# One burst for the next batch's packed product and two packed blocks, its columns inside an h tile

## The chip, the core and the metric

The kernel runs on one core of one Trainium2 chip. The metric is device time in microseconds of one execution; the median of three runs is 249.57 (249.48 to 250.11). The engines named below are TensorE (PE, with its weight loads PEld), VectorE (DVE), ScalarE (ACT), GpSimd (POOL) and SyncE (SP).

## The reference

Eight batches, eight heads, 576 positions, head size 64, 32 packed queries, a feed-forward layer of 512 to 2048 to 512:

```python
p_packed = sm_attn(p, k, v)                # softmax attention of 32 packed queries
out = sm_attn(q, p_packed, p_packed)       # attention of q over the 32 packed rows
x = out.transpose(0, 2, 1, 3).reshape(B * S, H * D)
h = x @ w_in
g = h * cos(h)
return g @ w_out
```

`sm_attn(qq, kk, vv)` is `softmax(scale * qq kk^T) vv`.

## The kernel before

For one batch `b` the kernel makes, in order:

- `s1(b)` (L142): scores of the packed queries against k, in two PSUM tiles, and their exp on ACT. `a1_xbar` (L158) or `a1_pe` (L163) transposes the result, `recips` (L152) takes reciprocals of its sums.
- `pp(b)` (L173), the packed product: 48 small matmuls (96 rows, 32 columns, 64 wide; L180) into 128 columns of a PSUM tile, and two copies to `pp_sb` in SBUF. `pp_T(b)` (L188) transposes it on PE (L192) and copies it to `ppT`, which has a buffer for each parity of `b`.
- `ppw(b, n)` (L195), a packed block: 8 matmuls (64 rows, 32 columns, 512 wide; L207) that multiply `ppT` by columns `512n` to `512n+511` of `w_in`, into both banks of a PSUM tile, and a cast into `PPW[b]` (L85 on ACT, L87 on DVE). There are four blocks, n = 0 to 3; `pw2(b, n)` (L485) makes two. Folding `w_in` into the packed rows spares the product `x @ w_in`.
- `s2(b)` (L221): scores of q against the packed rows (L137), exp on ACT (L225). `sums2` (L228) sums them with a matmul by ones and takes the logarithm; `normalise` (L238) makes the weights `a2n`.
- `h_mm(b, fc)` (L248) for fc = 0 to 15: one h tile, four matmuls (L254) of a 128-column piece of `PPW[b]` with `a2n[b]`. Its PSUM tile has two banks of 512 columns, of which each holds 288 (HS) used columns. ACT makes the cosine as a sine (L258), DVE multiplies (L261) into `gT`. The tiles of fc 4n to 4n+3 read block n.
- `out_gen(b)` (L331): `g @ w_out`, in chunks of 16 matmuls each (L339), whose result is copied to `osb` and stored by an SP DMA (L345). It is a generator: `fill(n)` (L355) issues its next n matmuls wherever it is called. These are the fillers, always those of the batch before. An odd batch has 80, an even one 64.

The whole order is written out by hand (a manual schedule): an instruction stands in its engine's queue where the program calls it. PE, ACT and DVE each run their queue in order.

`slot(s, hooks, keep, heavy)` (L471) is the h loop of batch s. It issues the 16 h tiles, spreads the fillers between them, and calls each hook after the h tile whose number it carries. An fc in `heavy` gets more fillers, half of them before its hook and half after.

PSUM has two single-bank buffers for the output tiles (pool `psO`, tile `ot`) and, from batch 1 on, three two-bank buffers (pool `psA`, `psa()`, L89) that score tiles, h tiles, packed products, transposes and packed blocks take in turn. A tile can be taken only when its buffer's last reader is done.

The bursts of small tiles in the loop over s = 3 to 6 (L545) are four for each batch: after `s2(s)` comes `ppw(s, 2)`; after `s1(s+1)` comes `ppw(s, 3)`; inside the slot, `pp(s+1)` stands after fc 5, with `pp_T(s+1)` after fc 6; and `pw2(s+1)`, blocks 0 and 1 of the next batch, after fc 10. The last batch, s = 7, has only its own two blocks. Batches 1 and 2 have slots of their own (L496, L542).

The diff touches `h_mm`, the hooks of the slots, and the calls around `pp(2)` and in the loop.

Of the kernel before, what the change touches and what calls it, by code (L numbers as in the profile page):

```python
# [15 lines left out]
def kernel(  # L16
# [18 lines left out]
    HS = S // 2  # L35
# [27 lines left out]
    V, ACT, G = nc.vector, nc.scalar, nc.gpsimd  # L63
# [25 lines left out]
    def psa(dt=FP32):  # L89
        return psum["A"].tile([128, 2, 512 if dt == FP32 else 1024], dt, name="psA", tag="A")  # L90
# [29 lines left out]
    def pack_p(b0, b1, flat=None):  # L120
        ng = 2 * (b1 - b0)
        if flat is None:
            flat = psa(BF16).rearrange("p a x -> p (a x)")
        for g in range(ng):
            nc.tensor.transpose(flat[:, g * 128:(g + 1) * 128],
                                p_bf[:, 2 * b0 + g].rearrange("p t d -> p (t d)"), ident)
        V.tensor_copy(out=P2[:, b0:b1].rearrange("p b h n -> p (b h n)"), in_=flat[:, 0:ng * 128])
# [14 lines left out]
    def s1(b):  # L142
        ps = scores(lambda r, h, e: P2[r, b, h, :], xT["k", b])
        sm = small.tile([128, 2], FP32, name="sums1")
        for y in range(2):
            ACT.activation(  # L146
                out=a1[b % 2][:, y, :, 0:TP].rearrange("p (e m) x -> p e m x", e=2),
                in_=ps[y][:, :, 0:HS].rearrange("p e (m x) -> p e m x", m=3),
                func=AF.Exp, scale=scale, accum_out=sm[:, y:y + 1])
        sums1[b] = sm  # L150
# [22 lines left out]
    def pp(b, eng=V, own=None):  # L173

        ps = own() if own else psa()[:, 0, :]
        for y in range(2):
            for j in range(C):
                c = 2 * (j % 3) + j // 3
                for x in range(4):
                    nc.tensor.matmul(ps[32 * x:32 * x + 32, y * D:(y + 1) * D],  # L180
                                     a1T[b][0:TP, y, j, 32 * x:32 * x + 32],
                                     bf["v", b][:, 2 * x + y, c * D:(c + 1) * D],
                                     start=(j == 0), stop=(j == C - 1))
        t = pp_sb[b % 2].rearrange("p a d -> p (a d)")
        copy(eng, t[:, 0:2 * D], ps[:, 0:2 * D])
        copy(eng, t[:, 2 * D:3 * D], ps[:, 0:D])
# [8 lines left out]
    def ppw(b, n, eng=None, own=False, later=False, cuts=((0, 512),)):  # L195
        if b not in PPW:
            PPW[b] = ppw_pool.tile([128, 2, DF], BF16, name="PPW", tag="PPW")
        two = isinstance(eng, tuple)
        if own:
            ps = [bank(), bank()]  # L200
        else:
            t = psa()
            ps = [t[:, 0, :], t[:, 1, :]]
        for x in range(4):
            for y in range(2):
                r = slice(64 * y, 64 * y + 64)
                nc.tensor.matmul(ps[y][32 * x:32 * x + 32, :], ppT[b % 2][r, 0, x, :],  # L207
                                 w_in_bf[r, x, n * 512:(n + 1) * 512], start=True, stop=True)

        def evacuate(cuts=cuts):  # L210
            if own or two:
                for a, z in cuts:
                    for y in range(2):
                        copy(eng[y] if two else eng, PPW[b][:, y, n * 512 + a:n * 512 + z], ps[y][:, a:z])
            else:
                copy(eng or (V, ACT)[n % 2], PPW[b][:, :, n * 512:(n + 1) * 512], t)
        if later:
            return [lambda c=c: evacuate((c,)) for c in cuts]
        evacuate()
# [25 lines left out]

    gT, joint = {}, {}

    def h_mm(b, fc):  # L248
        if fc == 0:
            g_tile(b)  # L250
        ps = psa()
        for y in range(2):
            for e in range(2):
                nc.tensor.matmul(ps[:, e, 0:HS], PPW[b][:, y, fc * 128:(fc + 1) * 128],  # L254
                                 a2n[b][:, y, e * HS:(e + 1) * HS], start=(y == 0), stop=(y == 1))
        cs = cos_pool.tile([128, S], BF16, name="cosT")
        csv = cs.rearrange("p (e x) -> p e x", e=2)
        ACT.activation(out=csv, in_=ps[:, :, 0:HS], func=AF.Sin, bias=PI_HALF)  # L258

        def rest():  # L260
            V.tensor_tensor(out=gT[b][:, fc, :].rearrange("p (e x) -> p e x", e=2),  # L261
                            in0=ps[:, :, 0:HS], in1=csv, op=ALU.mult)
            if fc % 8 == 7:
                j0 = (b % 2) * 64
                G.tensor_copy(out=joint[b // 2][:, fc - 7:fc + 1, j0:j0 + 64],  # L265
                              in_=gT[b][:, fc - 7:fc + 1, 512:576])
        return rest
# [18 lines left out]
    def h_rest(b):  # L286

        t = psa()
        for fc in range(NFC):
            for y in range(2):  # L290
                nc.tensor.matmul(t[:, fc // 8, (fc % 8) * 64:(fc % 8) * 64 + 64],
                                 PPW[b][:, y, fc * 128:(fc + 1) * 128], a2n[b][:, y, 512:576],
                                 start=(y == 0), stop=(y == 1))
        cs = cos_pool.tile([128, 2, 512], BF16, name="cosR", bufs=1)
        ACT.activation(out=cs, in_=t, func=AF.Sin, bias=PI_HALF)
        j0 = (b % 2) * 64
        V.tensor_tensor(out=joint[b // 2][:, :, j0:j0 + 64],
                        in0=t.rearrange("p a (f x) -> p (a f) x", x=64),
                        in1=cs.rearrange("p a (f x) -> p (a f) x", x=64), op=ALU.mult)
# [55 lines left out]
    def fill(n):  # L355
        while n > 0 and filler[1] > 0:
            next(filler[0])
            filler[1] -= 1
            n -= 1
# [111 lines left out]
    def slot(s, hooks, keep=0, heavy={}):  # L471
        left = filler[1] - keep
        weight = [1 + heavy.get(fc, 0) for fc in range(NFC)]
        for fc in range(NFC):
            h_mm(s, fc)()
            quota = (left * sum(weight[:fc + 1])) // sum(weight) - (left + keep - filler[1])
            first = quota
            while hooks and hooks[0][0] == fc:
                if first == quota and fc in heavy:
                    first = quota // 2  # L480
                    fill(first)
                hooks.pop(0)[1]()
            fill(quota - first if first != quota else quota)

    def pw2(b, n=0, eng=None):  # L485
        ppw(b, n, eng)
        ppw(b, n + 1, eng)

    def tk(n, b, i):
        return lambda: pe_T(n, b, (ACT, V, ACT), (i,))  # L490

    def cross(n, b):
        return lambda: xbar(n, b)

    osb_eng[0] = ACT
    slot(1, [(2, lambda: ppw(1, 2, (ACT, V))), (4, lambda: h_rest(0)),  # L496
             (5, lambda: ppw(1, 3, (ACT, V))), (6, lambda: pack_p(2, 4)), (8, tk("k", 2, 0)), (9, tk("k", 2, 1)),
             (9, cross("q", 2)), (10, tk("k", 2, 2)), (12, cross("k", 3))], 4, {4: 2})
    ACT.preload_act_table_set(EXP_SET)
    osb_eng[0] = V  # L500
    G.tensor_copy(out=gate, in_=xT["k", 3][0:1, 0, 0:1])
# [11 lines left out]
    recips(2)  # L513
    fill(5)
    pp(2)
    fill(2)
    pp_T(2)
    s1(3)
    a1_xbar(3)
    recips(3)  # L520
    fill(6)
    s2(2)
# [15 lines left out]
    for n, b in (("v", 4), ("q", 4), ("k", 5)):  # L538
        load(n, b)
    fill(9)  # L540
    osb_eng[0] = ACT
    slot(2, [(3, lambda: ppw(2, 2, (ACT, V))), (6, lambda: ppw(2, 3, (ACT, V))),  # L542
             (7, lambda: pp(3, ACT)), (8, lambda: pp_T(3, ACT)), (11, lambda: pw2(3))], 5, {11: 3})

    for s in range(3, B):  # L545
        nxt = s + 1 < B
        ACT.preload_act_table_set(EXP_SET)
        osb_eng[0] = V
        fill(1000)
        set_filler(s - 1)  # L550
        s2(s)
        ppw(s, 2, V)
        fill(8)
        if nxt:
            s1(s + 1)
            ppw(s, 3, V)
            a1_xbar(s + 1)
            xbar("q", s + 1)
            recips(s + 1)
            if s + 2 < B:  # L560
                xbar("k", s + 2)
                G.tensor_copy(out=gate, in_=xT["k", s + 2][0:1, 0, 0:1])
        else:
            ppw(s, 3, V)
        fill(4)
        sums2(s, 0)
        fill(5)
        sums2(s, 1)
        normalise(s)
        ACT.preload_act_table_set(SIN_SET)  # L570
        fill(13)
        osb_eng[0] = ACT
        for n, b in (("v", s + 2), ("q", s + 2), ("k", s + 3)):
            if b < B:
                load(n, b)
        slot(s, [(5, lambda: pp(s + 1, ACT)), (6, lambda: pp_T(s + 1, ACT)), (10, lambda: pw2(s + 1))] if nxt else [], 5, {10: 3})
    set_filler(B - 1)
    fill(1000)
    tail_chunk(B - 1, 4)
# [30 lines left out]
```

## Time and profile before

| what | value |
|---|---|
| median of three runs | 249.57 us |
| the profiled execution | 249.53 us |
| its span on the core | 247.6 us |
| granted TensorE clock over the span | 1.0 |
| L339, fillers | 482 and 47 recorded matmuls, 128.2 and 12.6 us busy |
| L254, h tiles | 448 matmuls, 73.2 us busy |
| L207, packed blocks | 224 and 32 matmuls, 10.4 and 1.6 us busy |
| L180, packed products | 336 and 48 matmuls, 4.0 and 0.6 us busy |
| L258, the sine of one h tile | 653 ns |
| L261, the multiply of one h tile | 757 ns |
| L87, a cast of a whole packed block on DVE | 1223 ns |
| L85, the same on ACT | 1012 ns |

A profile row reads: start, duration, engine, line, operation, output tile from input tiles, shape, count of merged instructions, and in brackets the idle time of the engine before them with what ended it. The duration of a merged row runs from its first start to its last end. Ends of matmuls are modelled, since they are pipelined; the distance of starts is firmer. A few matmul records are missing from the trace. All times are microseconds from the start of the span.

### The profile page before, as it was taken

What the parts mean: (1) busy time and instruction counts of PE and PEld (TensorE: products, weight loads), DVE (VectorE), ACT (ScalarE), POOL (GpSimd) and SP (SyncE); (2) the same over time, 40 slices, a digit from 0 to 9 for tenths busy, and PEclk for the clock granted to TensorE, in tenths of its full rate; (3) what the DMA queues carried; (4) which work ended last, traced back from release to release, by engine and by line L of the source; (5) the groups of instructions that cost most, each with busy time, mean ns of one, the idle gap of its engine ahead of it and who ended that gap; (6) DMA issues with size and microseconds to landing.
All of it is one profiled execution on the core that took longest, in us unless ns stands there. A gap on an engine that the chain in (4) does not pass through costs nothing.

```text
span 247.6 us, 5423 instructions
## 1 busy us (share of the span) xinstructions
PE 234.0 (95%) x2204; PEld 128.3 (52%) x2240; DVE 158.5 (64%) x244; ACT 170.3 (69%) x284; POOL 38.2 (15%) x61
## 2 busy tenths in 40 slices
PE   7988889999989999999999999999999999999993
PEld 3453344566445554565446554565456554665452
DVE  3369977676549777578757666578756685774000
ACT  2369998677568777888787677978886685874110
POOL 8532330200400041005000500030000000000000
PEclk9999999999999999999999999999999999999999
DMA  6999999999899999996999894989292113111123
GB/s 88 204 209 209 202 208 228 202 235 176 135 186 173 218 146 201 189 221 122 215 214 197 148 222 109 184 172 203 63 187 59 42 45 84 43 34 53 52 75 85
DMA packets 63992, 37.37 MB, mean 151 GB/s; under 512 B 36592, under 2 KB 59376, under 8 KB 63968
## 3 DMA queue, kind: packets, MB, share of 16 engines
q0 software_dynamic: 23184, 18.81, 50.0%
q1 hardware_dynamic: 40624, 18.09, 35.6%
q8 instruction: 17, 0.28, 0.5%
q10 hardware_dynamic: 160, 0.13, 0.2%
q14 instruction: 7, 0.06, 0.1%
HBM read 37.22 MB, written 9.44 MB: 188 GB/s over the span
## 4 chain that ended last, share of the span: by engine, by line
PE 82%; DMA 6%; DVE 4%; ACT 3%; issue 2%; POOL 2%; DVEq 0%; ACTq 0%; POOLq 0%
PE ot L339 48%; PE psA L254 22%; DMA w_in_bf<-in_moe_w_in_dram 6%; PE psA L207 3%; PE psA L137 2%; PE ot L325 1%; PE psA L233 1%; PE psA L180 1%; DVE gT L284 1%; PE psH L280 1%; DVE PPW L87 1%; ACT a2u L225 1%; DVE gT L261 1%; POOL kbf L94 1%; ACT L449 1%
## 5 line engine op out<-in xcount | busy, mean ns | idle before, releaser
L339 PE MATMUL ot<-w_out_bf,gT 128*128 128x512 bf16 x482 | 128.2, 379 | 2.8 <-issue 1.9
L261 DVE TENSOR_TENSOR gT<-psA,cosT 128x576 bf16<-128x576 f32 x112 | 83.5, 757 | 32.4 <-ACT cosT L258 31.5
L258 ACT ACTIVATE cosT<-psA 128x576 bf16<-128x576 f32 x112 | 73.0, 653 | 26.4 <-PE psA L254 24.8
L254 PE MATMUL psA<-a2n,PPW 128*128 128x288 bf16 x448 | 73.2, 286 | 0.0
L339 PEld LDWEIGHTS <-gT 128*128 128x128 bf16 x512 | 47.3, 98 | 43.5 <-issue 7.8
L254 PEld LDWEIGHTS <-PPW 128*128 128x128 bf16 x448 | 43.8, 98 | 30.5 <-issue 1.0
L87 DVE CAST PPW<-psA 128x1024 bf16<-128x1024 f32 (+1 forms) x25 | 26.1, 1050 | 7.7 <-PE psA L207 6.0
L87 DVE COPY osb<-ot 128x512 f32<-128x512 f32 (+1 forms) x14 | 9.4, 671 | 21.3 <-PE ot L325 17.4
L85 ACT COPY osb<-ot 128x512 f32<-128x512 f32 (+1 forms) x23 | 13.2, 575 | 13.5 <-PE ot L339 12.4
L265 POOL COPY joint<-gT 128x512 bf16<-128x512 bf16 x14 | 8.6, 617 | 88.4 <-DVE gT L261 88.4
L243 DVE SCALAR_TENSOR_TENSOR a2n<-a2u,r,lns 128x576 bf16<-128x576 bf16 x16 | 12.4, 814 | 8.1 <-ACT lns L241 8.1
L146 ACT ACTIVATE a<-psA 128x576 bf16<-128x576 f32 x16 | 10.3, 646 | 8.3 <-PE psA L137 8.3
L235 ACT ACTIVATE lns<-psA 128x576 f32<-128x576 f32 x16 | 10.3, 651 | 6.5 <-PE psA L233 5.9
L339 PE MATMUL ot<-w_out_bf,joint 128*128 128x512 bf16 x47 | 12.6, 379 | 0.1
L376 PE MATMUL ot<-wz 128*128 128x512 bf16 (+1 forms) x23 | 10.2, 548 | 2.0 <-DVE wz L390 1.7
L225 ACT ACTIVATE a2u<-psA,rs 128x576 bf16<-128x576 f32 x16 | 11.0, 738 | 1.5 <-PE psA L137 1.4
L207 PE MATMUL psA<-w_in_bf,ppT 64*32 64x512 bf16 x224 | 10.4, 380 | 0.2
L284 DVE TENSOR_TENSOR gT<-psH,cosT 128x512 bf16<-128x512 f32 x16 | 9.9, 682 | 0.4 <-ACT cosT L283 0.4
L241 ACT ACTIVATE lns<-lns 128x576 f32<-128x576 f32 x16 | 10.0, 674 | 0.0
L85 ACT CAST PPW<-psA 128x1024 bf16<-128x1024 f32 (+1 forms) x9 | 7.4, 825 | 2.8 <-PE psA L207 2.8
L283 ACT ACTIVATE cosT<-psH 128x512 bf16<-128x512 f32 x16 | 8.7, 619 | 0.9 <-issue 0.4
L280 PE MATMUL psH<-a2n,PPW 128*128 128x512 bf16 x30 | 7.9, 381 | 0.9 <-DVE PPW L87 0.6
(90 smaller groups left out, 163.8 us busy)
## 6 DMA issues: line engine op xcount, KB each, us to landing
kbf<-in_k_dram POOLq DMA_DIRECT2D x8, 576.0 KB, 13.5
vbf<-in_v_dram POOLq DMA_DIRECT2D x8, 576.0 KB, 7.4
qbf<-in_q_dram POOLq DMA_DIRECT2D x8, 576.0 KB, 10.6
out_dram<-osb SPq DMA_DIRECT2D x24, 192.0 KB, 2.8
out_dram<-osb SPq DMA_DIRECT2D x22, 128.0 KB, 2.9
w_in_bf<-in_moe_w_in_dram POOLq DMA_DIRECT2D x4, 512.0 KB, 16.6
w_out_bf<-in_moe_w_out_dram POOLq DMA_DIRECT2D x4, 512.0 KB, 21.2
out_dram<-osb SPq DMA_DIRECT2D x26, 64.0 KB, 2.1
```

The costliest lines, as they stand in the source:

```text
L85: ACT.copy(out=out, in_=in_)
L87: eng.tensor_copy(out=out, in_=in_)
L146: ACT.activation(out=a1[b % 2][:, y, :, 0:TP].rearrange("p (e m) x -> p e m x", e=2), in_=ps[y][:, :, 0:HS].rearrange("p e (m x) -> p e m ...
L207: nc.tensor.matmul(ps[y][32 * x:32 * x + 32, :], ppT[b % 2][r, 0, x, :], w_in_bf[r, x, n * 512:(n + 1) * 512], start=True, stop=True)
L225: ACT.activation(out=a2u[b][:, y].rearrange("p (e x) -> p e x", e=2), in_=ps[y][:, :, 0:HS], func=AF.Exp, scale=rs1[b][:, y:y + 1])
L243: V.scalar_tensor_tensor(out=a2n[b][:, y], in0=a2u[b][:, y], scalar=r1[b][:, y:y + 1], in1=lns[b][:, y], op0=ALU.mult, op1=ALU.mult)
L254: nc.tensor.matmul(ps[:, e, 0:HS], PPW[b][:, y, fc * 128:(fc + 1) * 128], a2n[b][:, y, e * HS:(e + 1) * HS], start=(y == 0), stop=(y == 1))
L258: ACT.activation(out=csv, in_=ps[:, :, 0:HS], func=AF.Sin, bias=PI_HALF)
L261: V.tensor_tensor(out=gT[b][:, fc, :].rearrange("p (e x) -> p e x", e=2), in0=ps[:, :, 0:HS], in1=csv, op=ALU.mult)
L280: nc.tensor.matmul(ps, PPW[b][:, y, fc * 128:(fc + 1) * 128], a2n[b][:, y, 0:512], start=(y == 0), stop=(y == 1))
L284: V.tensor_tensor(out=gT[b][:, fc, 0:512], in0=ps, in1=cs, op=ALU.mult)
L339: nc.tensor.matmul(pss[c], w, w_out_bf[:, fc, :], start=(fc == 0), stop=(fc == NFC - 1))
```

## The change

`h_mm` keeps a reference to the unused columns of the second bank of its newest tile, `ps[:, 1, HS:512]`, 224 columns wide. A new function `tiled(b, n)` calls `pp(b + 1, ACT)` with these columns in place of a PSUM tile of its own, and right behind it `pw2(b, n)`: blocks n and n+1 of the present batch.

In the loop over s, blocks 0 and 1 stand where 2 and 3 stood (after `s2(s)` and `s1(s+1)`), and `tiled(s, 2)` stands after fc 5; `pp_T(s+1)` moves from fc 6 to fc 7, and the heavy fc becomes 5 in place of 10. The hook with `pw2(s+1)` is gone. In the last batch, blocks 1 to 3 follow each other after the first eight fillers.

In slot 2, blocks 2 and 3 of batch 2, which stood after fc 3 and fc 6, join `pp(3)` after fc 7; `pp_T(3)` moves from fc 8 to fc 9; `pw2(3)` is gone and the heavy fc becomes 7. In slot 1 blocks 2 and 3 are made together after fc 3, `h_rest(0)` (the last 64 columns of batch 0) moves from fc 4 to fc 6 and `pack_p(2, 4)` from fc 6 to fc 7, and the heavy fc becomes 3. Before slot 2, `s1(3)` and `a1_xbar(3)` stand directly behind `pp(2)`, ahead of two fillers and `pp_T(2)`.

The numbers of matmuls, casts and copies are unchanged.

```diff
+    spare = [None]
+
     def h_mm(b, fc):
         if fc == 0:
             g_tile(b)
         ps = psa()
+        spare[0] = ps[:, 1, HS:512]
...
+    def tiled(b, n):
+        pp(b + 1, ACT, own=lambda: spare[0])
+        pw2(b, n)
+
...
-    slot(1, [(2, lambda: ppw(1, 2, (ACT, V))), (4, lambda: h_rest(0)),
-             (5, lambda: ppw(1, 3, (ACT, V))), (6, lambda: pack_p(2, 4)), (8, tk("k", 2, 0)), (9, tk("k", 2, 1)),
-             (9, cross("q", 2)), (10, tk("k", 2, 2)), (12, cross("k", 3))], 4, {4: 2})
+    slot(1, [(3, lambda: pw2(1, 2, (ACT, V))), (6, lambda: h_rest(0)), (7, lambda: pack_p(2, 4)), (8, tk("k", 2, 0)), (9, tk("k", 2, 1)),
+             (9, cross("q", 2)), (10, tk("k", 2, 2)), (12, cross("k", 3))], 4, {3: 2})
...
     pp(2)
+    s1(3)
+    a1_xbar(3)
     fill(2)
     pp_T(2)
-    s1(3)
-    a1_xbar(3)
...
-    slot(2, [(3, lambda: ppw(2, 2, (ACT, V))), (6, lambda: ppw(2, 3, (ACT, V))),
-             (7, lambda: pp(3, ACT)), (8, lambda: pp_T(3, ACT)), (11, lambda: pw2(3))], 5, {11: 3})
+    slot(2, [(7, lambda: tiled(2, 2)), (9, lambda: pp_T(3, ACT))], 5, {7: 3})
...
         s2(s)
-        ppw(s, 2, V)
+        ppw(s, 0, V)
         fill(8)
         if nxt:
             s1(s + 1)
-            ppw(s, 3, V)
+            ppw(s, 1, V)
...
         else:
-            ppw(s, 3, V)
+            for n in range(1, 4):
+                ppw(s, n, V)
...
-        slot(s, [(5, lambda: pp(s + 1, ACT)), (6, lambda: pp_T(s + 1, ACT)), (10, lambda: pw2(s + 1))] if nxt else [], 5, {10: 3})
+        slot(s, [(5, lambda: tiled(s, 2)), (7, lambda: pp_T(s + 1, ACT))] if nxt else [], 5, {5: 3})
```

## The prediction

> **What bounds the kernel now.** I read the engine table of the page first, then its chain of waits, then the timeline around each burst of small tiles.
>
> ```profile
> PE 234.0 (95%) x2204; PEld 128.3 (52%) x2240; DVE 158.5 (64%) x244; ACT 170.3 (69%) x284; POOL 38.2 (15%) x61
> PE 82%; DMA 6%; DVE 4%; ACT 3%; issue 2%; POOL 2%; DVEq 0%; ACTq 0%; POOLq 0%
> ```
>
> TensorE (PE) is busy 95% of the span and is 82% of the chain that ends last: from 38 us on, a microsecond in which PE does nothing is a microsecond of the kernel. So I count only PE's starts. Next, the timeline of slot 5 (batch 5's h loop), around its packed product (L180):
>
> ```profile
> 160.74 2.98 DVE L261 TENSOR_TENSOR gT<-psA,cosT 128x576 bf16<-128x576 f32 x4 [0.24 <-ACT cosT L258]
> 161.57 1.36 ACT L258 ACTIVATE cosT<-psA 128x576 bf16<-128x576 f32 x2 [0.27 <-PE psA L254]
> 161.59 0.65 PE L254 MATMUL psA<-a2n,PPW 128*128 128x288 bf16 x4
> 162.17 0.48 PEld L180 LDWEIGHTS <-a1T 96*32 96x32 bf16 x48 [0.24 <-issue]
> 162.22 0.55 PE L180 MATMUL psA<-vbf,a1T 96*32 96x64 bf16 x48
> 162.93 0.38 PE L339 MATMUL ot<-w_out_bf,gT 128*128 128x512 bf16 x1 [0.16 <-issue]
> ```
>
> Two rates: a group of eight L339 fillers takes 1.89 and one 0.38, so one starts every (1.89-0.38)/7 = 0.216; four L254 take 0.65, one 0.286, so an h tile occupies PE for 4 x 0.121 = 0.485. The h tile of fc 5 starts at 161.59, so the next matmul is due at 162.07; after L180 the filler starts at 162.93. The product alone costs 0.86 (0.82 in slot 4). The first line is the VectorE multiply: the last of its four is that of fc 5 and ends at 163.72, well after L180 has run. Then the two packed blocks (L207) further on:
>
> ```profile
> 167.14 0.81 PE L339 MATMUL ot<-w_out_bf,gT 128*128 128x512 bf16 x3
> 167.88 0.62 PE L207 MATMUL psA<-w_in_bf,ppT 64*32 64x512 bf16 x16
> 168.69 1.22 DVE L87 CAST PPW<-psA 128x1024 bf16<-128x1024 f32 x1
> 169.09 0.65 PE L254 MATMUL psA<-a2n,PPW 128*128 128x288 bf16 x4
> ```
>
> Due 167.14 + 3 x 0.216 = 167.79; after the burst three fillers (0.65) precede the L254 at 169.09, so it resumes at 168.44: cost 0.65.
>
> **The merged burst.** Apart, product and pair cost 0.84 + 0.65 = 1.49. Together: 0.48 for the 48 L180 (the weight loads' length), 0.56 for the pair (167.88 to 168.44), and between them 0 to 0.16 (the idle that L339 shows after L180); I take 0.06, nearer to none, since L137 and L207 follow each other without a gap in the bursts after `s2` (149.38 and 149.63 in slot 5), though both of those have 64 rows: 1.10 from the first L180 to the next filler. With an entry of 0.12 (0.15 in slot 5, 0.10 in slot 4) that is 1.22, a gain of 0.27 a batch, between 0.17 and 0.33. The Trainium skill (TensorEngine Tiling (Array Packing), Key Properties) says a change of tiling mode, not of tile, drains TensorE; L180 has 96 rows and L207 64, so by the rule the inner boundary stays and the upper end, 0.16, holds: 0.17 a batch. No row here has the two side by side, so no run yet shows it.
>
> **The wait that it adds.** The product no longer has a tile of its own; it writes columns 288 to 415 of the second bank of the fc-5 h tile, which L258 and L261 read. In the order of the built changed kernel the first L180 still waits for VectorE, and the copies out of its columns (`pp_sb`, ScalarE) now wait for VectorE too, where before they waited for PE alone. So I take the wait to be for the L261 of the same h tile. Read by addresses alone the columns would be free at once. The Trainium skill (PSUM — Partial Sum Buffer, section PSUM bank collisions raise a hardware error) has the rule to guard by bank and quadrant, not by address, which speaks against the change; no row of before shows such a pair of accesses. By the rule the sum below stands, by addresses rival A does. How fast a matmul follows such a release is in slot 2:
>
> ```profile
> 83.45 0.76 DVE L261 TENSOR_TENSOR gT<-psA,cosT 128x576 bf16<-128x576 f32 x1 [0.27 <-ACT cosT L258]
> 84.26 0.55 PE L180 MATMUL psA<-vbf,a1T 96*32 96x64 bf16 x48 [0.27 <-DVE gT L261]
> 84.97 0.38 PE L339 MATMUL ot<-w_out_bf,gT 128*128 128x512 bf16 x1 [0.16 <-issue]
> ```
>
> The multiply ends at 84.21, L180 starts at 84.26: 0.05. So in slot 5 L180 may start at 163.77, 1.70 after the due time 162.07. In slot 4:
>
> ```profile
> 134.11 0.65 PE L254 MATMUL psA<-a2n,PPW 128*128 128x288 bf16 x4
> 135.48 0.76 DVE L261 TENSOR_TENSOR gT<-psA,cosT 128x576 bf16<-128x576 f32 x1 [0.17 <-ACT cosT L258]
> ```
>
> Due 134.59, free 136.24 + 0.05: 1.70 again. It is the latency of sine and multiply, not a backlog. The half quota of the heavy fc is issued before the product: 3 fillers in slots 3 and 5, 5 in slots 4 and 6, 4 in slot 2 (fc 7). PE then stands for 1.70 - 0.65 = 1.05, 1.70 - 1.08 = 0.62 and 1.70 - 0.86 = 0.84. Behind L180 in PE's queue stand the pair, the fillers and the next h tile: all late.
> - Slots 3, 5: 1.05 + 1.10 - 1.49 = +0.66 each. The next h tiles come with a transpose tile between them: fc 8 takes the buffer of fc 6, free 2.19 after fc 6 began (161.59 to 163.77), and is due 2 x 0.485 + 3 x 0.216 + 0.12 = 1.74 after: +0.45. Gone are two waits of before: the transposes for the multiply of fc 5 (0.14) and an h tile behind the 1.22 cast that ends at 169.91 (0.17). Net +0.80.
> - Slots 4, 6: 0.62 + 1.10 - 1.47 = +0.25 (two more fillers hide the rest).
> - Slot 2: before, single blocks 0.53 and 0.44, the product 1.15 with its wait, the pair 0.66: 2.78. After: 0.84 + 1.10, plus fc 8 waiting for block 2's cast (0.49 + 1.22 + 0.05 after L207 began at 0.48, so 2.24, against due at 1.10 + 0.86): 0.28, plus fc 10 for the multiply of fc 8: 0.25. 2.47, so -0.31.
>
> **Moved work.** Blocks 0 and 1 of a batch go to the bursts after `s2` and `s1`, where 2 and 3 stood: same matmuls, same casts, nothing. The last batch makes three blocks in one burst where it made one. The one costs 0.45 (205.25 due, 205.70 resumed), each more 0.20 (pair less single): +0.40; their casts, 2 x 1.22 on VectorE, stand ahead of an `osb` copy and `a2n`, about 0.1 too late: +0.5 (0.4 to 0.6). Slot 1: two singles 0.90 become a pair 0.65: -0.25; but `h_rest`, moved from fc 4 to fc 6, holds its buffer long:
>
> ```profile
> 46.63 1.10 PE L291 MATMUL psA<-a2n,PPW 128*128 128x64 bf16 x32
> 48.82 1.23 DVE L297 TENSOR_TENSOR joint<-psA,cosR 128x1024 bf16<-128x1024 f32 x1 [1.41 <-ACT cosR L295]
> ```
>
> It is free 3.47 after it began (46.63 to 50.05, and 0.05); before, 3.38 of PE work came in between, now 0.93 + 3 fillers + h tile + p transposes 0.25 + 2 fillers = 2.75: +0.63. Slot 1: +0.35 (-0.25 to +0.9, if the k transposes wait as well). `s1(3)` next to `pp(2)`, ahead of fillers and `pp_T(2)`: one boundary less, -0.1 (-0.3 to 0). SP's and POOL's queues keep their order except that the score transpose `a1_xbar(3)` goes ahead of two output stores; nothing on the path waits for it.
>
> **Sum:** 2 x 0.80 + 2 x 0.25 - 0.31 + 0.5 + 0.35 - 0.1 = +2.5. The profiled execution took 249.53 (span 247.6, 1.9 around it), 0.04 below the median 249.57: 252.1. With the inner boundary at 0 and the other terms at their low ends it is 2.1 - 5 x 0.06 - 0.31 + 0.4 - 0.25 - 0.3 = +1.3; with 0.16 and the high ends 2.1 + 5 x 0.10 - 0.31 + 0.6 + 0.9 = +3.8.
>
> **Rivals.**
> - A, faster: the product waits for nothing as late as its own multiply. Four batches gain 0.27 each, slot 2 0.84 - 0.12 more (-1.03), the rest stays +0.75: -1.4, 248.2. It decides from six fillers ahead of L180 (6 x 0.216 + 0.12 + 0.27 = 1.69): with them the stall is paid by the boundary. For it: the product reads and writes nothing that L258 and L261 touch. Against: the wait in the built order and at most 5 fillers. 0.17.
> - B, no change: VectorE or ScalarE set the slot's pace, PE would have stood later anyway, and slots 3 to 6 come out even: 250.0. For it: VectorE 0.757 an h tile against PE's 0.485 + 1.5 x 0.216 = 0.81. Against: the same 1.70 at both densities of fillers. 0.11.
> - C, dearer: the late casts and multiplies push further h tiles, in slots 1, 2 and 7 too, by half a microsecond in five slots: 252.1 + 2.4 = 254.5. For it: only three score buffers. Against: waits found above are all under 0.5. 0.07.
> - Forecast: 0.65.
>
> Differences of 0.3% (0.75 us) are what can be told from none. Slower 0.65 + 0.07 = 0.72, same 0.11, faster 0.17. The range reaches from B's edge to short of C: 249.5 to 253.8.
>
> **What would show it.** In slots 3 to 6, L180 with idle "<-DVE gT L261" of some 0.9 and 0.5, starting 0.05 after the multiply's end; L207 directly behind; L339 1.10 after the first L180. The burst after s1 in the last batch has 24 L207. If L180 starts within 0.2 of its due time, the forecast falls; if it waits and the time still falls, burst boundaries are worth more than 0.27.

## The result and the profile after

| kernel | median, us | range | runs |
|---|---|---|---|
| before | 249.45 | 249.25 to 250.11 | 6 |
| after | 254.05 | 253.08 to 254.22 | 6 |

The change makes the kernel slower by 1.73% (ratio 1.0173, 95% interval 1.0153 to 1.0193), 4.6 us. The direction is the forecast's; the size is nearly twice its 2.5 and lies 0.25 above the upper end of the range. The profiled execution took 254.08 with a span of 252.3.

The first fence is from the page of the changed kernel: the row of each engine (busy time, share of the span, instructions), and the share of each engine in the chain that ends last.

```profile
PE 236.6 (94%) x2240; PEld 128.9 (51%) x2240; DVE 159.7 (63%) x244; ACT 169.2 (67%) x282; POOL 38.1 (15%) x61
PE 77%; DVE 7%; ACT 5%; issue 1%; ACTq 0%; DVEq 0%
```

TensorE still sets the end. Its share of the chain falls from 82% to 77%, and VectorE's rises from 4% to 7%, but such shares prove little: a second trace of the kernel before (experiment 5) has 79% and 3%. What TensorE stands for is read from the timeline. Note the first count as well: 2240 matmuls here, 2204 before, though the change adds none. It is 36 records that the first trace lacked, and one of the prediction's terms hung on one of them (below).

The timeline of slot 5 in the changed kernel shows where it stands (start, duration, engine, line, operation, operands, count, idle before). Lines from L255 on are three higher than before: L257 is the h tile, L261 its sine, L264 its multiply, L342 a filler.

```profile
163.38 2.98 DVE L264 TENSOR_TENSOR gT<-psA,cosT 128x576 bf16<-128x576 f32 x4 [0.25 <-ACT cosT L261]
...
164.23 0.65 PE L257 MATMUL psA<-a2n,PPW 128*128 128x288 bf16 x4
...
164.72 0.81 PE L342 MATMUL ot<-w_out_bf,gT 128*128 128x512 bf16 x3
165.46 0.09 PEld L180 LDWEIGHTS <-a1T 96*32 96x32 bf16 x1 [0.42 <-issue]
166.41 0.55 PE L180 MATMUL psA<-vbf,a1T 96*32 96x64 bf16 x48 [0.88 <-DVE gT L264]
...
166.90 0.62 PE L207 MATMUL psA<-w_in_bf,ppT 64*32 64x512 bf16 x16
...
167.45 0.82 PE L342 MATMUL ot<-w_out_bf,gT 128*128 128x512 bf16 x3
...
170.35 0.65 PE L257 MATMUL psA<-a2n,PPW 128*128 128x288 bf16 x4 [0.34 <-DVE gT L264]
```

The first weight load of the product is done at 165.55, and its matmul starts at 166.41, 0.05 after the four merged multiplies end (163.38 + 2.98 = 166.36). The h tile of fc 5 began at 164.23, so after four matmuls (0.485) and three fillers (0.65) the product was due at 165.36: it stood for 1.05. Then the burst runs without a stop: pair 0.49 behind the first L180, filler 1.04 behind it. The last row is the h tile of fc 8, which waits for the multiply of fc 6. In slot 4 five fillers cover more, and the product stands for 0.62:

```profile
137.65 0.76 DVE L264 TENSOR_TENSOR gT<-psA,cosT 128x576 bf16<-128x576 f32 x1 [0.17 <-ACT cosT L261]
...
138.46 0.55 PE L180 MATMUL psA<-vbf,a1T 96*32 96x64 bf16 x48 [0.45 <-DVE gT L264]
```

Over the whole kernel, the view of line L180 lists what ended TensorE's idle time before its instructions, in us, with the number of times (idle time counts from the modelled end of the matmul before, so a wait shows 0.17 shorter than by starts):

```profile
its engine sat idle before it (us, times) until:
...
  DVE gT L264: 3.3, 5
```

To see where each microsecond went I cut the span at the start of the first h tile of each slot; a stage is a slot and the preparation of the next batch behind it. These numbers are differences of start times in the two traces. The forecast column sums the prediction's terms by stage.

| stage | before | after | change | forecast |
|---|---|---|---|---|
| up to slot 1 | 40.71 | 41.47 | +0.76 | 0 |
| slot 1, prep 2 | 35.26 | 35.44 | +0.18 | +0.25 |
| slot 2, prep 3 | 28.08 | 28.02 | -0.06 | -0.31 |
| slot 3, prep 4 | 25.23 | 26.52 | +1.29 | +0.80 |
| slot 4, prep 5 | 28.34 | 28.83 | +0.49 | +0.25 |
| slot 5, prep 6 | 25.23 | 26.25 | +1.02 | +0.80 |
| slot 6, prep 7 | 28.10 | 29.12 | +1.02 | +0.75 |
| slot 7 and end | 36.67 | 36.64 | -0.03 | 0 |

So the changed part costs 3.9 and the forecast had 2.5 for it. The other 0.76 lies ahead of every changed instruction: TensorE's transposes of the k rows of batch 1 waited for their DMA. First before, then after:

```profile
16.68 0.50 PE L112 MATMUL ot<-ident,kbf 96*128 96x96 bf16 x8
```

```profile
17.69 0.51 PE L112 MATMUL ot<-ident,kbf 96*128 96x96 bf16 x8 [0.99 <-DMA kbf<-in_k_dram]
```

The same wait stands in six of the ten traces of this study, and one of the six is the second trace of the kernel before (experiment 5), whose slot 1 starts at 41.42, 0.71 later than in the first:

```profile
17.64 0.51 PE L112 MATMUL ot<-ident,kbf 96*128 96x96 bf16 x8 [0.88 <-DMA kbf<-in_k_dram]
```

Over the ten traces slot 1 starts anywhere from 40.71 to 42.94, also in kernels that are the same up to there, and no edit lies ahead of it. So a start later by nearly 0.76 comes without the change too, and I judge the edits by the stages after it. The fastest runs of the two kernels, 249.25 and 253.08, lie 3.83 apart, about what the changed part costs.

### The profile page after: what moved, and what is told of

Read it like the earlier page. It is cut to its first block, busy times and chain, and to the rows that moved or that the text cites. A ratio compares the mean times of both kernels' runs of the same rounds, so it can differ in the third digit from the quotient of the medians.

```text
span 252.3 us, 5463 instructions
## 1 busy us (share of the span) xinstructions
PE 236.6 (94%) x2240; PEld 128.9 (51%) x2240; DVE 159.7 (63%) x244; ACT 169.2 (67%) x282; POOL 38.1 (15%) x61
## 4 chain that ended last, share of the span: by engine, by line
PE 77%; DVE 7%; ACT 5%; issue 1%; ACTq 0%; DVEq 0%
PE ot L342 45%; PE psA L257 21%; DVE gT L264 3%; PE psA L207 3%; ACT cosT L261 2%; PE psA L137 2%; DVE PPW L87 1%; PE ot L328 1%; PE psH L283 1%; PE psA L180 1%; PE psA L233 1%; DVE gT L287 1%; ACT a2u L225 1%; ACT L452 1%; DVE joint L300 0%
## 5 line engine op out<-in xcount | busy, mean ns | idle before, releaser
L342 PE MATMUL ot<-w_out_bf,gT 128*128 128x512 bf16 x512 | 132.9, 379 | 0.0
L264 DVE TENSOR_TENSOR gT<-psA,cosT 128x576 bf16<-128x576 f32 x112 | 83.2, 757 | 32.5 <-ACT cosT L261 31.5
L261 ACT ACTIVATE cosT<-psA 128x576 bf16<-128x576 f32 x112 | 72.6, 653 | 26.2 <-PE psA L257 24.5
L257 PE MATMUL psA<-a2n,PPW 128*128 128x288 bf16 x448 | 73.2, 286 | 1.8 <-DVE gT L264 1.0
L342 PEld LDWEIGHTS <-gT 128*128 128x128 bf16 x512 | 47.9, 98 | 43.5 <-issue 7.5
L257 PEld LDWEIGHTS <-PPW 128*128 128x128 bf16 x448 | 43.7, 98 | 33.0 <-issue 3.4
L87 DVE CAST PPW<-psA 128x1024 bf16<-128x1024 f32 (+1 forms) x25 | 26.9, 1094 | 13.8 <-PE psA L207 11.7
L342 PE MATMUL ot<-w_out_bf,joint 128*128 128x512 bf16 x48 | 13.0, 379 | 0.0
L207 PE MATMUL psA<-w_in_bf,ppT 64*32 64x512 bf16 x224 | 9.8, 379 | 0.1
L180 PEld LDWEIGHTS <-a1T 96*32 96x32 bf16 x384 | 4.0, 95 | 6.7 <-issue 5.8
```

The costliest lines, as they stand in the source:

```text
L87: eng.tensor_copy(out=out, in_=in_)
L342: nc.tensor.matmul(pss[c], w, w_out_bf[:, fc, :], start=(fc == 0), stop=(fc == NFC - 1))
```

## The experiments

The theory: TensorE stands because the product's columns lie in the h tile of the same fc, in one of its two PSUM banks, and the multiply of that tile must end first; and merging product and pair spares too little to pay for it. The rivals: the merged burst is itself dear, or VectorE and ScalarE, with two casts at once, hold the slot back.

**1. A tile of its own for the product (e_own) and a single bank of its own (e_bank).** Both leave the merged burst where it is and change only where the product's columns lie: in a tile of the three-buffer pool, or in one of the two banks of the output tiles. The first diff is e_own's, the second e_bank's.

```diff
-        pp(b + 1, ACT, own=lambda: spare[0])
+        pp(b + 1, ACT)
```

```diff
-        pp(b + 1, ACT, own=lambda: spare[0])
+        pp(b + 1, ACT, own=bank)
```

> The changed kernel, with the packed product of the merged burst in a score buffer of its own instead of the h tile's free columns; all else as changed. Wait theory: the first L180 is no longer held by the multiply of its own h tile (0.88 us of idle in slot 5, some 0.45 in slot 4), but the third tile of the burst, the second packed block, takes the buffer of that h tile and waits for it, about 0.2 us in slots 3 and 5, nothing in 4 and 6. Slot 5 to the next h loop: 25.5 (before 25.23, changed 26.25); slot 4: 28.2 (28.34, 28.83); the whole about 250 (249.5 before, 254.05 changed). Rival, the burst itself is dear (mode change inside): slot 5 stays near 26.2 and the whole near 253.5. Rival, the late blocks (cast just ahead of the tiles that need them) cost the time: the same, 253.5.

> The changed kernel, with the packed product of the merged burst in one of the two output-tile banks; all else as changed. Wait theory: L180 waits for a copy that is long done, the two blocks take the buffers of the two h tiles before, so no tile of the burst waits for the multiply of the h tile just ahead: L180 within 0.15 us of its due time in slots 3 to 6; slot 5 25.2 to 25.3, slot 4 28.2; the whole 249.2, no difference from before that can be told. Rival, the burst itself or the late blocks are dear: 253 or more. A wait could come instead at the next output chunk, whose bank the product shares: then idle of L342 for the copies of pp_sb.

e_own: 250.35 (249.43 to 251.49), ratio 1.0009 (0.9987 to 1.0030). e_bank: 249.24 (248.91 to 250.30), ratio 0.9982 (0.9967 to 0.9997). Stages of slots 2 to 6: 27.22, 25.48, 28.25, 25.48, 28.55 for e_own; 27.23, 25.23, 28.25, 25.23, 28.55 for e_bank. Timeline of slot 5, e_own:

```profile
163.09 0.56 PE L180 MATMUL psA<-vbf,a1T 96*32 96x64 bf16 x48
163.57 0.88 PE L207 MATMUL psA<-w_in_bf,ppT 64*32 64x512 bf16 x16
...
164.04 0.11 PEld L207 LDWEIGHTS <-ppT 64*32 64x32 bf16 x7 [0.36 <-issue]
```

and e_bank:

```profile
162.21 0.56 PE L180 MATMUL ot<-vbf,a1T 96*32 96x64 bf16 x48
...
162.70 0.63 PE L207 MATMUL psA<-w_in_bf,ppT 64*32 64x512 bf16 x16
...
166.10 0.65 PE L257 MATMUL psA<-a2n,PPW 128*128 128x288 bf16 x4 [0.28 <-DVE gT L264]
```

No L180 row carries idle time any more. In e_own the pair takes 0.88 in place of 0.63, because its second block is now the one that needs the buffer of the fc-5 tile; there is a stall of 0.25, not of 1.05. In e_bank nothing in the burst waits. From after to e_bank the stages of slots 2 to 6 lose 0.79, 1.29, 0.58, 1.02 and 0.57, together 4.25: with the same burst, the same casts and the same order, the place of 128 columns is worth all that the change cost and a little more. That disposes of the rivals. Both edits take the product out of the shared bank and out of the shared tile at once, so no run tells which of the two makes it wait. What e_bank leaves is the wait of fc 8 (0.28 of idle time, 0.44 by starts), which eats what the merge and the end of two waits of before (0.31) spare: its slots 3 and 5 are as long as before.

**2. Other work ahead of the product (e_hide, e_hide2) and none (e_none).** If the stall is a fixed latency of 1.70, fillers moved ahead of it must shrink it one for one. The heavy fc issues half its quota before the hook; e_hide (first diff) issues all of it, e_none (second) nothing.

```diff
-                    first = quota // 2
+                    first = quota // 2 if s == 1 else quota
```

```diff
-                    first = quota // 2
+                    first = quota // 2 if s == 1 else 0
```

> The changed kernel with the whole quota of fillers of the heavy h tile ahead of the merged burst in slots 2 to 6, none behind it (before: half and half). Wait theory: the idle before L180 falls by the fillers' time, from 0.88 to about 0.3 in slots 3 and 5 and to nothing in 4 and 6; some comes back at the h tiles that wait for the casts of the blocks, now without fillers in between (fc 6 to 8, 0.3 each; slot 2's fc 8 about 1.1). Whole: 252 (251.5 to 253). Rival, burst or late blocks: no better than 254, or worse.

> The changed kernel with none of the heavy h tile's fillers ahead of the merged burst in slots 2 to 6, all behind it. Wait theory: the idle before L180 becomes 1.5 us in every slot (1.70 less the entry), so +0.65 in slots 3 and 5, +1.08 in 4 and 6, +0.86 in slot 2, less up to 0.8 in slots 3 and 5 and 0.6 in slot 2, where the tiles after the burst no longer wait: whole about 256.3 (255 to 258). Rivals: fillers are only moved by a few tiles, so no change, 254.

e_hide: 255.83 (255.52 to 256.76), ratio 1.0245 (1.0221 to 1.0268); the expectation missed. e_none, one run: 257.51, inside what was expected. Its slots 3 and 5 are 0.65 longer than in the changed kernel and its slots 4 and 6 1.08 longer, which is three and five fillers; the time that the expectation took back in slots 3 and 5 did not come back. Slot 5 in e_none:

```profile
165.06 2.98 DVE L264 TENSOR_TENSOR gT<-psA,cosT 128x576 bf16<-128x576 f32 x4 [0.24 <-ACT cosT L261]
...
168.09 0.55 PE L180 MATMUL psA<-vbf,a1T 96*32 96x64 bf16 x48 [1.53 <-DVE gT L264]
```

and in e_hide:

```profile
167.81 0.55 PE L180 MATMUL psA<-vbf,a1T 96*32 96x64 bf16 x48 [0.24 <-DVE gT L264]
...
171.98 0.38 ACT L85 COPY ppT<-psA 128x256 bf16<-128x256 bf16 x1
...
172.41 0.77 PE L257 MATMUL psA<-a2n,PPW 128*128 128x288 bf16 x5 [1.00 <-ACT ppT L85]
```

The stall itself does what the theory says: idle time 1.53 without fillers ahead, 0.88 with three, 0.24 with six, a filler's 0.216 for each. But e_hide gives the time back at another place: a wait of 1.00 at the h tile right behind `pp_T`, which needs the buffer that ScalarE's copy to `ppT` must leave first. The cause is an edit that did more than was meant: a line behind the hook reads "no half was issued" from `first == quota` and issues the quota a second time, so the later h tiles stood without fillers between them. e_hide2 mends that line.

```diff
-            fill(quota - first if first != quota else quota)
+            fill(quota - first if fc in heavy else quota)
```

> The changed kernel with the whole quota of the heavy h tile ahead of the merged burst in slots 2 to 6 and none behind it, the quota issued once (in e_hide it was issued twice, ahead and behind, and the next h tiles stood without fillers). Wait theory: idle before L180 0.3 in slots 3 and 5 (before: 0.88), none in 4 and 6; fc 7 then waits 0.28 for the cast, fc 8 0.17 for the multiply of fc 6 in place of 0.5 to 0.8; slot 2's fc 8 waits 1.2. Slot 5 25.5 (changed 26.25), slot 4 28.6 (28.83), the whole 252.0 (changed 254.05). Rival, the wait is only moved to other tiles: 253.5 or more.

Measured: 252.42 (252.26 to 252.49), ratio 1.0110 (1.0095 to 1.0125), some 0.6 points better than after. The timeline of e_hide2, the h tile of fc 8 in slot 2, then product and fc 8 in slot 5:

```profile
87.17 0.66 PE L257 MATMUL psA<-a2n,PPW 128*128 128x288 bf16 x4 [1.14 <-DVE PPW L87]
...
165.02 0.55 PE L180 MATMUL psA<-vbf,a1T 96*32 96x64 bf16 x48 [0.24 <-DVE gT L264]
...
168.61 0.65 PE L257 MATMUL psA<-a2n,PPW 128*128 128x288 bf16 x4 [0.37 <-DVE gT L264]
```

Slot 4 came out at 28.60 as expected, slot 5 at 25.90 where 25.5 was: with no filler left behind the burst, fc 8 waits 0.53 (I had 0.17; its sine stands behind the 1.01 cast on ScalarE), and in slot 2 fc 8 stands 1.14 for the cast of block 2. Fillers ahead of the product are fillers missing behind it, and both sides have a wait to hide; e_bank, which removes the wait, is 1.3 points better than e_hide2, which hides it.

**3. The old order in slot 1 (e_slot1).** On top of e_bank, the hooks of slot 1 are those of before.

```diff
-    slot(1, [(3, lambda: pw2(1, 2, (ACT, V))), (6, lambda: h_rest(0)), (7, lambda: pack_p(2, 4)), (8, tk("k", 2, 0)), (9, tk("k", 2, 1)),
-             (9, cross("q", 2)), (10, tk("k", 2, 2)), (12, cross("k", 3))], 4, {3: 2})
+    slot(1, [(2, lambda: ppw(1, 2, (ACT, V))), (4, lambda: h_rest(0)),
+             (5, lambda: ppw(1, 3, (ACT, V))), (6, lambda: pack_p(2, 4)), (8, tk("k", 2, 0)), (9, tk("k", 2, 1)),
+             (9, cross("q", 2)), (10, tk("k", 2, 2)), (12, cross("k", 3))], 4, {4: 2})
```

> e_bank with the hooks of slot 1 as they were before the change. The h_rest theory: its buffer is held for 3.47 us after it begins, so that in the changed order fc 8 stands 0.74 for it; with the old order that idle goes, two single blocks come back for a pair (+0.25). Slot 1 with what follows to the next h loop 34.9 (before 35.26, e_bank 35.45), since s1(3) behind pp(2) gives 0.3 to 0.4; the whole 248.7 (e_bank 249.24). Rival, the pair gives more than h_rest costs: 249.5.

Its slot 1 took 35.02, against 35.45 in e_bank: the edit to slot 1 costs 0.43. The whole, 249.39 (248.39 to 250.84), ratio 0.9981 (0.9961 to 1.0001), misses the expected 248.7 and can't be told from before; in its trace slot 1 started at 42.94, two microseconds later than in e_bank, and that scatter hides 0.43. What slot 1 waits for in the changed kernel:

```profile
50.09 1.10 PE L294 MATMUL psA<-a2n,PPW 128*128 128x64 bf16 x32
...
52.28 1.22 DVE L300 TENSOR_TENSOR joint<-psA,cosR 128x1024 bf16<-128x1024 f32 x1 [0.55 <-ACT cosR L298]
...
53.56 0.65 PE L257 MATMUL psA<-a2n,PPW 128*128 128x288 bf16 x4 [0.58 <-DVE joint L300]
```

`h_rest` holds its buffer from 50.09 to the end of its multiply at 53.50, and the h tile that is next in turn for it starts 0.06 later.

**4. Both waits away (e_best).** On top of e_slot1 the transpose `pp_T` gets a single bank as well, so that it no longer takes a turn in the three-buffer pool, and in slot 2 product and pair move one fc earlier.

```diff
-    slot(2, [(7, lambda: tiled(2, 2)), (9, lambda: pp_T(3, ACT))], 5, {7: 3})
+    slot(2, [(6, lambda: tiled(2, 2)), (8, lambda: pp_T(3, ACT, own=bank))], 5, {6: 3})
...
-        slot(s, [(5, lambda: tiled(s, 2)), (7, lambda: pp_T(s + 1, ACT))] if nxt else [], 5, {5: 3})
+        slot(s, [(5, lambda: tiled(s, 2)), (7, lambda: pp_T(s + 1, ACT, own=bank))] if nxt else [], 5, {5: 3})
```

> e_slot1 with pp_T of the slots in an output-tile bank too, so that no score buffer is taken between fc 7 and fc 8, and the merged burst of slot 2 after fc 6 in place of fc 7. Wait theory: fc 8 of slots 3 and 5 no longer waits for the multiply of fc 6 (0.44 each), slot 2's waits of 0.33 and 0.29 go: slot 5 24.8, slot 2 26.7; slots 4 and 6 as they were or up to 0.2 worse, if pp_T waits for an osb copy. The whole 247.5 (247.0 to 248.3), faster than both kernels.

Measured: 247.11 (246.98 to 249.15) against 249.63 for before, measured beside it, ratio 0.9921 (0.9891 to 0.9950): faster than both kernels. From its page, and from the timeline of slot 5:

```profile
PE 236.2 (96%) x2240; PEld 129.0 (52%) x2240; DVE 159.7 (65%) x244; ACT 168.9 (68%) x282; POOL 38.1 (15%) x61
```

```profile
162.35 0.56 PE L180 MATMUL ot<-vbf,a1T 96*32 96x64 bf16 x48
...
165.46 0.28 PE L192 MATMUL ot<-ident,pp_sb 128*128 128x128 bf16 x2
...
165.79 0.65 PE L257 MATMUL psA<-a2n,PPW 128*128 128x288 bf16 x4
```

No row carries idle time, product and transposes write `ot`, and the wait of fc 8 (the last row) is gone. Slots 2 to 6 take 26.65, 24.79, 28.24, 24.78 and 28.53, against 28.08, 25.23, 28.34, 25.23 and 28.10 before. All but the last are shorter; the last has the three-block burst behind it.

**5. The kernel before once more (e_before).** e_bank's slots 5 and 4 came out 0.14 and 0.16 longer than the prediction's own prices give without the stall (-0.27 + 0.44 - 0.31 = -0.14, measured 0.00; -0.25, measured -0.09). The suspect was a record: in the first trace the filler behind every product had a weight load, but its matmul row came one filler late.

> The kernel before, once more, for its records. Missing-record theory: in the first profile the filler right behind each L180 had a weight load but no matmul record, so that I read 0.22 too much into the product's burst; with the record there, the distance from the last L180 to the next L339 is about 0.14, and the product alone costs 0.62 to 0.64. Rival: the 0.36 is real, and the record never existed.

One run, 250.64. First the row of the first trace that had made me doubt (the matmul row behind it, at 162.93 with a count of one, is in the prediction), then the second trace at the same place:

```profile
162.69 0.11 PEld L339 LDWEIGHTS <-gT 128*128 128x128 bf16 x2
```

```profile
163.32 0.55 PE L180 MATMUL psA<-vbf,a1T 96*32 96x64 bf16 x48
...
163.80 0.61 PE L339 MATMUL ot<-w_out_bf,gT 128*128 128x512 bf16 x2
```

Two weight loads, but one matmul, in the first; two matmuls in the second. There the first filler stands 0.48 behind the first L180, not 0.71. The page of the second trace counts as many matmuls as weight loads:

```profile
PE 237.1 (95%) x2240; PEld 128.0 (51%) x2240; DVE 158.4 (64%) x244; ACT 170.2 (68%) x284; POOL 38.2 (15%) x61
```

From slot 1 on the stages agree between the two traces within 0.02, but for slot 3, where the second one's product waited for a DMA (25.64 against 25.23).

## Why the prediction was right in direction and short in size

**The wait: right, within 0.01.** Forecast: 1.05 in slots 3 and 5, 0.62 in 4 and 6, 0.84 in 2. By starts: 1.05 in slot 5, 0.62 in slot 4, 0.83 in slot 2, each 0.05 behind the multiply. e_none shows the full 1.70, e_bank shows it gone. The rule of the Trainium skill (PSUM — Partial Sum Buffer, section PSUM bank collisions raise a hardware error), to guard by bank and quadrant and not by address, is in accord: in the changed kernel TensorE waits though its product touches no column that the multiply reads. What the runs show is the order as built and its price; whether it goes by bank or by the whole tile they don't show, and no run tried the two accesses at once.

**The merged burst: nearly right.** 1.10 was forecast from the first L180 to the filler, and 1.04 was measured: 0.35 from the first to the last L180, 0.13 to the first L207, 0.56 for the pair. The 0.48 that the forecast took for the product already held the change of shape behind it, so the 0.06 between product and pair was counted on top.

**The failing step: "The product alone costs 0.86 (0.82 in slot 4)."** In slot 5 it costs 0.63: 0.48 from the first L180 to the filler, as in e_before, and 0.15 at its entry. The other 0.22 was one filler at 0.216, which ran and left no matmul row; I took the hole for idle time at the burst's exit. So product and pair apart cost 0.63 + 0.65 = 1.28 in slot 5 and 0.60 + 0.65 = 1.25 in slot 4, not 1.49 and 1.47. The merge costs 1.04 and an entry of 0.09 (in e_bank the first L180 starts 0.31 behind a filler that takes 0.216), so it spares 0.12 to 0.15, not 0.27. With that term mended, slots 3 and 5 are 1.05 + 1.04 - 1.28 + 0.50 (fc 8) - 0.31 (the two old waits) = +1.00, and slot 5 measured +1.02; slot 4 is 0.25 + 0.22 = +0.47 against +0.49; slot 2 is -0.31 + 0.22 = -0.09 against -0.06. Five bursts at 0.22 make 1.1 of the 1.4 that the forecast was short in the changed part; with them the sum would have been +3.6 in place of +2.5. The sign of the error was to be seen in the same trace: the engine row has 2240 weight loads and 2204 matmuls, and the row behind L180 has two loads and one matmul.

The rule of the Trainium skill (TensorEngine Tiling (Array Packing), Key Properties), that a change of mode drains, gave 0.17 a batch and is nearer than the value I took. The trace of after agrees with it: the last L180 and the first L207 start 0.13 apart, as far as the last L180 and the next filler in e_before. The page has no price for it; these rows do.

**The other terms.** fc 8 in slot 5 waited 0.51 (forecast 0.45), the cast and fc 10 in slot 2 cost 0.33 and 0.29 (0.28 and 0.25). The three-block burst: slot 6 less slot 4 in e_bank, each against before, +0.45 less -0.09, 0.54 (0.5). Slot 1: +0.43 by e_slot1 (+0.35); `s1(3)` behind `pp(2)`: 35.02 less 35.26, -0.24 (-0.1).

**What stays open.** Slot 3 cost 0.27 more than slot 5: fc 8 waited 0.78 there, because the sine of fc 6 started 2.73 behind the first L180, not 2.45 as in slot 5. The same 0.78 is in e_none; in e_own and e_bank both slots have 0.44. Why the sine was late was not found. Open too is whether the product waits because of the shared bank or the shared tile. How much of the 4.6 between the two medians is the scatter of the start can't be read from the times alone; the traces give the change 3.9.

**The rivals.** A fell (L180 waits). B fell: with the wait removed slots 3 and 5 come out even, but because the wait of fc 8 takes back 0.44, not because VectorE sets the pace; e_best takes that wait away and the slots shorten by 0.45. C, 254.5, is near the time, but not by its mechanism: slots 1, 2 and 7 have no late h tiles beyond those of the forecast, and the last stage is as long as before. Only the longer wait of fc 8 in slot 3 is of its kind. Against C the prediction had said that all waits found were under 0.5, which passed over its own 0.63 for `h_rest`.

## What to carry to other kernels

Free columns in a tile that another engine is still reading were not a free buffer here: the tile that borrowed them inherited the host tile's whole latency (sine and multiply, 1.70), and everything behind it in TensorE's queue with it. A separate bank cost nothing here and took the wait away; only after that is the merging of bursts worth measuring, and it was worth 0.12 to 0.15 a batch. Before an idle gap in a trace is priced, count the records on both sides of it: more weight loads than matmuls means that the gap may be work.

## What the runs showed of the hardware that was not expected

- A change between two small tile shapes inside a burst costs as much as going back to the full array: 0.13 between starts at both, in after and e_before. Putting two bursts of different shape side by side therefore saves one such change, not two.
- The start of slot 1 varied by 2.2 us between executions (40.71 to 42.94), with the landing of early transfers (in six of ten traces TensorE waits 0.8 to 1.0 for the k rows), which is more than most edits here were worth; comparing stages told effects of 0.1 apart that whole times did not.
